# A new order for the list of steps of a banded-attention and mixture-of-experts kernel

## The chip, the cores and the metric

The kernel runs on one core of a Trainium2 chip. A core has five engines that work side by side, each through its own instructions in order: TensorE (PE in the profile, PEld for its weight loads), VectorE (DVE), ScalarE (ACT), GpSimd (POOL) and SyncE (SP). Loads and stores are issued by a queue of POOL, SP or ACT and are carried by 16 DMA engines. The metric is device time in microseconds (us), the median of several executions.

## The reference

Eight batches, eight heads, 576 positions, head size 64. Attention looks back at most 63 positions; its output, heads side by side, is the input of a layer of experts that is chosen once per batch by a gate on the mean over the positions.

```python
scores = scale * np.matmul(q, k.transpose(0, 1, 3, 2))     # (8, 8, 576, 576)
mask = (rel >= 0) & (rel < 64)                             # rel = row - column
attn = softmax(np.where(mask, scores, -1e9))
x = np.matmul(attn, v)                                     # heads side by side: (8, 576, 512)
...
pooled = x.mean(axis=1)
logits = pooled @ w_gate                                   # 8 experts
e_idx = np.argmax(logits, axis=1)                          # one expert for a batch
h = np.maximum(x[mask] @ w1[e], 0.0)                       # w1: 512 x 1024
out[mask] = gate_w[mask, None, None] * (h @ w2[e])         # w2: 1024 x 512
```

## The kernel before

Everything is issued from one list of short names, `OPS`. The loop at the end of the kernel walks through it and calls one function for each name, and no other scheduling takes place. The list therefore sets the order of instructions on every engine and in every queue: an engine works through its own steps in the order in which they stand in the list, and where a step has to wait, all that stands behind it on the same engine waits too.

The attention of a batch is cut into five units: four pairs of heads over the first 512 positions ("main" units, numbers 5b to 5b+3 for batch b) and one unit for the last 64 positions of all heads (the "tail", number 5b+4). The names, with unit or batch number behind the letter:

- `Q` loads q (even number 2b) or k (odd, 2b+1) of batch b on POOL's queue, cast to bf16 on the way, 512 KB as stored. For batch 0 a suffix names a range of heads (`Q0.48` is q, heads 4 to 7). `Y` loads two heads in fp32 on SP and `C` casts them. `t` loads both tails (two DMAs on POOL). `L` loads a fifth of a batch's v on POOL, `L5b` to `L5b+3` 128 KB each and `L5b+4` the tail, and `V` makes the copy of v that is shifted by 64 positions (two VectorE copies, lines 150 and 151).
- `T` transposes q and k of a unit on TensorE, `U` and `k` copy the transposed q and k out of PSUM, `S` makes the scores, `E` the exponential on ScalarE. The band mask is either a factor, `K` (VectorE, line 297), or, where the name of S has a `b` (`Sb`, `Smb`), two products on TensorE that add a large negative number first (line 269).
- `l` makes the row sums on TensorE, `n` and `R` their logarithm and reciprocal on ScalarE, `A` the product with v, `X` its scaling on VectorE with the sum for the mean.
- `g` and `j` are the gate's product, `G` its maximum and index on VectorE (line 404), `H` and `I` the gate's weight. `P` reads the index into a register of POOL; only then can `W4b` and `W4b+1` (the halves of w1, columns 0 to 511 and 512 to 1023) and `W4b+2` and `W4b+3` (the halves of w2) be loaded, 512 KB each as stored.
- `c` is the next piece of the expert layer on TensorE. They come in a fixed order, 18 for a batch, and this text counts them from c0: c(18b) to c(18b+7) are the eight column blocks of w1 (line 461; the first four need `W4b`, the others `W4b+1`), c(18b+8) is its tail (line 470), then two halves for each of four row blocks of w2 (line 503; the first half needs `W4b+2`, the second `W4b+3`), and the tail (line 512). `ra` or `rd` evacuates the oldest piece that is done, on ScalarE or on VectorE; `O` stores the oldest finished output on POOL's queue, `o` on SP's (the tail's second half then on ACT's).

A letter `a` or `d` inside a name picks ScalarE or VectorE for a copy; an `m` lets T, S or A use one of the three PSUM buffers of the expert layer in place of its own one. The row sums of all units and the gate share one PSUM buffer (`lb`), so an `l` waits until `n` has read the one before. q and k have buffers for three batches, the weights for three, v for three.

POOL's queue carries all loads of q, k, v and the weights and nearly all stores. Its order before, up to the weights of batch 0, is: Q0.48 Q1.48 Q0.2 Q1.2 Q3 t0 Q2 L0 L3 L1 L2 L4 t1 Q4 L9 Q5 L5 L7 L8 L6 t2 Q6 Q7 P0 W0 L12 W1 W2 L13 W3 L11 L14 L10.

## Time and profile before

| | us |
|---|---|
| median of 3 executions (203.06 to 203.96) | 203.13 |
| profiled execution, first to last instruction (span) | 201.9 |
| TensorE busy | 183.5 |
| ScalarE busy | 131.8 |
| VectorE busy | 119.9 |
| POOL busy | 111.0 |
| first expert product (c0) starts | 40.84 |
| last expert product ends | 197.6 |

The profile gives the span of the execution that it was taken from, and not its device time; the median of the executions stands 1.2 us above that span. In its rows the first number is the start or the busy time in us, then come engine, source line, operation, and the tiles written and read; "x40" counts instructions, and brackets tell how long the engine sat idle and what ended that. Rows of DMA issues give size and the time from issue to landing. Busy time of TensorE includes the pipelining of its products, so it is not a measure of how well it is used; the start-to-start distance of products is.

### The profile page before, as it was taken

How to read it: one execution, taken by the hardware profiler on the slowest of the kernel's cores; microseconds unless marked ns; L12 is line 12 of the kernel's file. 1: busy time of each engine (PE TensorE's matmuls, PEld its weight loads, DVE VectorE, ACT ScalarE, POOL GpSimd, SP SyncE). 2: the span in 40 equal slices, each digit the busy share in tenths (PEclk: the TensorE clock that was granted, in tenths of full speed). 3: DMA queues.
4: the chain of work that ended last, by engine and by line, in shares of the span. 5: the costliest groups of instructions: out<-in, count | busy, mean ns of one | idle time of the engine just before them, and what ended most of it. 6: DMA issues, size and time to landing. Idle time of an engine off the chain costs nothing.

```text
span 201.9 us, 8105 instructions
## 1 busy us (share of the span) xinstructions
PE 183.5 (91%) x3518; PEld 124.2 (62%) x3522; DVE 119.9 (59%) x347; ACT 131.8 (65%) x247; POOL 111.0 (55%) x158
## 2 busy tenths in 40 slices
PE   0487886899999999999999999999999999999991
PEld 0455564656677756577667666676656666776760
DVE  3527989595477546895877457966494651216410
ACT  2179998876599578977779975757787436321121
POOL 7985939235931593478633552439452716553561
PEclk9999999999999999999999999999999999999998
DMA  6999999999999999999999999999999999999693
GB/s 135 175 188 159 194 162 198 199 198 174 196 201 197 170 198 193 174 201 167 200 206 200 169 195 223 259 208 137 183 237 243 266 254 212 274 212 301 235 325 134
DMA packets 83346, 41.16 MB, mean 204 GB/s; under 512 B 48080, under 2 KB 80976, under 8 KB 83312
## 3 DMA queue, kind: packets, MB, share of 16 engines
q0 software_dynamic: 81936, 39.72, 138.5%
q1 hardware_dynamic: 768, 0.85, 1.3%
q8 instruction: 27, 0.44, 0.8%
q10 hardware_dynamic: 608, 0.08, 0.2%
q14 instruction: 7, 0.06, 0.1%
HBM read 61.88 MB, written 9.44 MB: 353 GB/s over the span
## 4 chain that ended last, share of the span: by engine, by line
PE 77%; DMA 9%; POOL 7%; issue 3%; DVE 2%; ACT 1%; POOLq 0%; DVEq 0%; ACTq 0%
PE ph L461 28%; PE po L503 25%; DMA vw<-in_v_dram 9%; PE tp L225 5%; PE ph L470 4%; PE s L275 4%; PE av L331 3%; PE po L512 3%; PE lb L309 3%; POOL vw L141 2%; POOL km L110 2%; POOL qm L110 1%; POOL out_dram L492 1%; PE gps L392 1%; POOL qkt L133 1%
## 5 line engine op out<-in xcount | busy, mean ns | idle before, releaser
L503 PE MATMUL po<-w2b,hm 128*64 128x512 f16 x512 | 60.1, 379 | 0.0
L461 PE MATMUL ph<-xm,w1b 128*64 128x512 f16 x512 | 60.0, 379 | 0.0
L461 PEld LDWEIGHTS <-w1b 128*64 128x64 f16 x512 | 31.7, 110 | 18.7 <-issue 0.4
L503 PEld LDWEIGHTS <-hm 128*64 128x64 f16 x512 | 30.1, 110 | 19.3
L141 POOL DMA_DIRECT2D vw<-in_v_dram x32 | 28.9, 910 | 13.3 <-DMA w1b<-in_moe_w_dram 4.3
L446 ACT ACTIVATE hm<-ph,gw 128x512 f16<-128x512 f32 x39 | 26.6, 693 | 13.4 <-PE ph L461 13.3
L492 POOL DMA_DIRECT2D out_dram<-ob x31 | 17.2, 557 | 25.0 <-DMA w1b<-in_moe_w_dram 7.0
L351 ACT ACTIVATE ln<-lb 128x512 f32<-128x512 f32 (+1 forms) x40 | 22.5, 563 | 11.8 <-PE lb L309 8.6
L364 DVE CUSTOM_DVE_ANT_0 xm<-av,rl 128x512 f16<-128x512 f32 x32 | 21.6, 686 | 10.4 <-PE av L331 9.5
L482 ACT COPY ob<-po 128x512 f32<-128x512 f32 x18 | 10.6, 586 | 23.6 <-PE po L503 23.6
L448 DVE TENSOR_SCALAR hm<-ph,gw 128x512 f16<-128x512 f32 x25 | 18.7, 748 | 12.1 <-PE ph L461 11.6
L357 ACT ACTIVATE rl<-ln 128x512 f32<-128x512 f32 (+1 forms) x40 | 23.3, 594 | 1.5 <-DVE pool L364 1.3
L225 PE MATMUL tp<-ident,qm 128*64 128x128 bf16 x256 | 13.8, 232 | 7.4 <-DMA qm<-in_q_dram 6.9
L288 ACT ACTIVATE pe<-s 128x1024 f16<-128x1024 f32 x19 | 19.5, 1028 | 1.4 <-PE s L275 0.7
L297 DVE TENSOR_TENSOR pe<-pe,mask 128x1024 f16<-128x1024 f16 x24 | 16.3, 687 | 3.9 <-ACT pe L288 3.1
L252 ACT COPY kT<-tp 128x512 bf16<-128x512 bf16 x19 | 11.2, 597 | 9.0 <-PE tp L225 8.0
L225 PEld LDWEIGHTS <-qm 128*64 128x64 bf16 x256 | 10.7, 118 | 10.0 <-DMA qm<-in_q_dram 6.9
L482 DVE COPY ob<-po 128x512 f32<-128x512 f32 x14 | 9.7, 690 | 10.7 <-PE po L503 10.5
L423 POOL DMA_DIRECT2D w1b<-in_moe_w_dram x16 | 12.6, 785 | 5.9 <-DMA vw<-in_v_dram 2.9
L275 PEld LDWEIGHTS <-kT 64*128 64x128 bf16 x576 | 10.1, 95 | 8.9 <-issue 5.6
L331 PEld LDWEIGHTS <-vw 128*64 128x64 f16 x512 | 12.4, 112 | 4.7 <-issue 1.2
L225 PE MATMUL tp<-ident,km 128*64 128x128 bf16 x256 | 13.9, 231 | 1.4 <-DMA km<-in_k_dram 0.9
(80 smaller groups left out, 267.2 us busy)
## 6 DMA issues: line engine op xcount, KB each, us to landing
w1b<-in_moe_w_dram POOLq DMA_DIRECT2D x16, 512.0 KB, 9.3
w2b<-in_moe_w_dram POOLq DMA_DIRECT2D x16, 512.0 KB, 13.4
out_dram<-ob POOLq DMA_DIRECT2D x31, 256.0 KB, 8.1
vw<-in_v_dram POOLq DMA_DIRECT2D x32, 128.0 KB, 9.0
km<-in_k_dram POOLq DMA_DIRECT2D x7, 512.0 KB, 9.3
qm<-in_q_dram POOLq DMA_DIRECT2D x7, 512.0 KB, 9.0
out_dram<-obt POOLq DMA_DIRECT2D x14, 64.0 KB, 7.7
qkt<-in_q_dram POOLq DMA_DIRECT2D x8, 64.0 KB, 7.6
```

Of the source, the lines that this page charges most:

```text
L141: nc.gpsimd.dma_start(out=vt[:, 2 * J + 1], in_=v[b, :, 128 * J:128 * J + 128].rearrange("h c d -> c h d"))
L225: nc.tensor.transpose(tp[p0:p0 + 64, n, r], t[:, 2 * i + hh, ts(r, 64)], ident)
L288: nc.scalar.activation(out=po, in_=sp[0], func=AF.Exp, scale=scale)
L351: nc.scalar.activation(out=ln, in_=lb[:, 0:n], func=AF.Ln)
L357: nc.scalar.activation(out=rl, in_=lns.pop((b, i)), func=AF.Exp, scale=-1.0)
L364: nc.vector.tensor_tensor_reduce(out=xm[:, i], in0=av.rearrange("q r p -> q (r p)"), in1=rl, scale=1.0, scalar=0.0, op0=ALU.mult, op1=ALU.add,
L446: nc.scalar.activation(out=o, in_=i, func=AF.Relu, scale=g)
L448: nc.vector.tensor_scalar(out=o, in0=i, scalar1=g, scalar2=0.0, op0=ALU.mult, op1=ALU.max)
L461: nc.tensor.matmul(out=ph[64 * c:64 * c + 64], lhsT=w1t[:, kb, ts(2 * ft + c, 64)], rhs=xm[:, kb], start=(kb == 0), stop=(kb == 3), skip_g ...
L482: copy(e)(out=ob, in_=po)
L492: (nc.scalar if n and eng is nc.sync else eng).dma_start(out=dst, in_=src)
L503: nc.tensor.matmul(out=po[64 * c:64 * c + 64], lhsT=hm[:, fb, ts(2 * r + c, 64)], rhs=w2t[:, fb], start=(fb == 0), stop=(fb == 7), skip_gr ...
```

## The change

The list is replaced by another one with the same steps; nothing else in the kernel changes. Every step of before is there once, with these differences: nine S with mask products on TensorE become three (units 0, 7 and 9), and their units, with others exchanged, get a `K` (37 in place of 31); 12 evacuations go from `ra` to `rd` (ra 65 to 53, rd 47 to 59); ten `U` go from VectorE to ScalarE, two `k` the other way; one of the two casts C goes to ScalarE; nine S and two A less, and one T more, use the expert layer's PSUM; three stores go from POOL's queue to SP's (`o` 2 to 5).

The order on every engine is new. On POOL, up to the weights of batch 0 and a little beyond: Q0.48 Q1.48 (identity) t0 Q1.2 Q2 (band) Q0.2 Q3 L2 L1 L3 L0 Q5 L4 t1 Q4 L7 L5 L8 L6 Q7 t2 P0 W0 L9 W1 Q6 L13 L10 L11 L12 W2 W3. Stores begin between W9 and L22 of that queue, where before they began behind W17.

```diff
 OPS = (
-    "Y0.24 Q0.48 Q1.48 Q0.2 Cd0.24 y i Q1.2 Y1.24 Q3 Cd1.24 z Tm3 Tm2 mb T0 Tm1 ka3 ka2 ka0 "
-    "t0 Ud3 Ud2 Q2 Sb3 L0 L3 ka1 L1 L2 E3 Smb2 L4 Ud0 l3 Ud1 t1 S0 T4 E2 kd4 Ud4 n3 Smb1 E0 "
-    "Mb K0 E1 R3 Q4 L9 Tm5 Sb4 Tm7 Tm8 Ud5 Q5 ka5 kd8 E4 L5 kd7 l1 n1 T6 l4 n4 Ud7 l2 Sb5 ka6 "
-    "n2 R1 R4 l0 V0 A3 Ud6 L7 Am1 n0 E5 T9 X3 Am2 Ud9 S7 R2 L8 E7 Ud8 X1 R0 l5 X2 L6 n5 Smb6 "
-    "A0 Am4 K7 ka9 E6 t2 X4 X0 Sb8 l7 g0 n7 T12 j0 Q6 Sm9 Tm10 G0 Ud12 kd12 E8 Ud10 H0 E9 "
-    "Tm13 Tm11 R7 K9 l6 R5 ka10 Sb12 Ud11 ka13 V1 n6 Q7 l8 P0 Ud13 W0 I0 kd11 T14 Am5 A7 X7 "
-    "A6 Ud14 kd14 L12 n8 X5 E12 R6 l12 n12 Sm14 X6 S11 l9 E14 Smb10 Tm17 E11 n9 T18 W1 Ud17 "
-    "A9 W2 E10 S13 kd18 Ud18 L13 Tm15 Ud15 l10 Am8 R8 W3 kd15 ka17 T16 K14 L11 c X8 L14 n10 "
-    "E13 R9 c ra X9 c R10 c rd c g1 K11 rd S17 j1 G1 ra ra c H1 L10 c rd l14 K13 c t3 ra c P1 "
-    "n14 Q8 ra c c rd c V2 Ua16 c c ra ka16 l11 A10 X10 Am12 W4 c Q9 R12 X12 n11 ra W5 R11 "
-    "A11 rd W6 T19 E17 c l13 n13 R13 Ua19 I1 X11 c Sm18 S15 K17 L15 rd E18 W7 R14 A13 c l17 "
-    "ra X13 A14 c L16 L17 X14 g2 n17 Tm20 E15 ra kd19 c Ud20 ra L18 kd20 T22 S19 Sm16 E19 L19 "
-    "j2 G2 c P2 t4 K15 E16 Q10 K18 c ra c W8 H2 ra ka22 c ra c c S20 l18 ra rd rd K16 c n18 "
-    "Q11 K19 L21 ra Tm21 c c Ua21 Ud22 l16 W9 T23 R17 kd21 L23 V3 c c R18 c ra Am17 Ud23 n16 "
...
-    "I6 l39 W27 R38 c n39 O O A38 rd R39 c W25 W26 ra X39 X38 g7 c j7 O c G7 c ra c P7 rd ra "
-    "c c O W29 O c ra c O rd H7 O ra c O c W28 W31 ra O ra O c ra c c ra rd c c c c rd c W30 "
-    "I7 O ra O c rd c c ra rd O c O O rd c O rd O O c rd c c O ra c c rd c O rd ra rd c c O "
-    "rd O c c ra O O c c c c ra rd o O c ra O c ra o "
+    "Q0.48 Q1.48 Y1.24 i t0 Tm3 Q1.2 Ua3 Ca1.24 kd3 Tm2 Y0.24 T4 Q2 Cd0.24 Ud2 Sm3 y ka2 Tm1 "
+    "Q0.2 mb E3 Ud1 ka1 S2 Tm0 E2 K3 Q3 kd4 Ua0 kd0 Sm1 l3 z Sb0 K2 E1 n3 Ud4 L2 Tm7 L1 L3 L0 "
+    "Q5 l2 E0 T5 ka7 L4 K1 t1 Tm6 Ua7 Mb n2 l1 Q4 R3 kd6 S4 Ua5 L7 kd5 n1 V0 Smb7 E4 l0 L5 R2 "
+    "A3 Ud6 K4 L8 T8 n0 X3 L6 E7 Am2 R0 S5 l4 Q7 A1 E5 Am4 Am0 X2 X0 n4 S6 Ud8 R4 l7 kd8 T9 "
+    "Tm13 K5 R1 X4 n7 l5 Tm12 E6 X1 g0 S8 n5 ka9 R7 E8 Tm11 ka13 j0 Ud12 K6 G0 R5 H0 Ua9 l6 "
+    "Ua13 t2 kd12 V1 Ua11 A7 K8 Sm12 T10 P0 S13 n6 l8 X7 A5 E12 E13 kd11 kd10 Ud10 W0 n8 L9 "
+    "Smb9 W1 Q6 E9 R6 I0 T14 X5 S10 Am6 L13 A8 K12 X6 l12 R8 c E10 L10 c c rd ka14 n12 L11 K10 "
+    "l9 R12 rd n9 R9 c c L12 K13 l10 W2 X8 S11 ra Am9 rd W3 c ra n10 c Q8 X9 Ua14 g1 j1 rd G1 "
+    "E11 rd H1 K11 P1 c S14 ra R10 Tm17 Tm18 Ua17 l11 kd17 T15 Ua18 E14 V2 c Ud15 S17 ka18 Am10 "
+    "n11 kd15 A12 c X12 W4 ra Q9 l13 E17 T16 Am13 K14 t3 n13 S18 l14 A11 X10 c rd R13 W5 c c "
+    "n14 c L14 E18 Ud16 ra X13 c kd16 t4 c c R11 rd K18 K17 c l17 X11 rd W6 S16 n17 c E16 W7 I1 "
+    "c T19 rd c ka19 rd l18 ra R14 rd c Tm23 ra Ua19 c n18 A14 Ud23 ka23 L16 ra c X14 ra g2 L17 "
+    "c K16 j2 c Tm21 R17 G2 S15 L15 rd c ra E15 Ud21 kd21 L18 P2 c S19 c rd T24 Tm20 c K15 E19 "
+    "ka20 c L20 Q10 S21 rd H2 Q11 l16 V3 A17 c Ua20 ka24 c R18 X17 Ua24 n16 W8 T22 A18 I2 l15 "
+    "rd E21 L19 R16 K19 rd Sm20 L24 K21 L23 n15 S23 X18 c E20 A16 c X16 K20 Ua22 W9 E23 l19 O "
+    "rd ka22 c n19 Tm26 T28 Ud26 c ra kd26 l20 Ud28 kd28 n20 S26 ra Am19 R19 R15 X19 c A15 T27 "
+    "X15 l21 L22 rd E26 ka27 n21 c rd c K23 R21 L21 S24 c K26 ra E24 V4 c t5 K24 S22 l23 ra R20 "
+    "ra c c g3 ra n23 c Ud27 W10 W11 l24 n24 ra A21 ra X21 c T29 Am20 c ra kd29 j3 Q12 O G3 E22 "
+    "H3 Ua29 c R23 c I3 S28 l26 X20 Q13 E28 c c L27 R24 A24 P3 K22 X24 L28 Am23 n26 S27 l22 ra "
+    "E27 c X23 c ra A22 W12 n22 c K27 Tm25 rd ra L26 Ud25 T32 ka25 Tm30 L25 W13 W15 S29 kd30 "
+    "E29 Ud30 c c ra K28 L29 R26 R22 ra V5 W14 c X22 c rd l27 n27 g4 kd32 S25 Ua32 ra c A26 j4 "
+    "E25 c G4 T31 H4 rd S32 Ud31 X26 K29 l28 R27 c rd n28 A27 c ra R28 I4 L35 c c rd E32 kd31 c "
+    "O ra l29 L31 S30 K25 rd n29 c c t6 ra c X27 c A28 l25 P4 n25 Q14 c c ra E30 T33 c R25 ka33 "
+    "K30 ra L30 W16 rd c l30 S31 R29 Ua33 Am25 O L33 T34 K32 X28 W17 c rd Ud34 Q15 A29 ra n30 "
+    "X25 c E31 c c X29 S33 l32 n32 g5 rd rd L32 kd34 c E33 O T36 O W18 c W19 rd j5 O Ua36 c L36 "
+    "V6 O A32 rd R32 S34 kd36 t7 T35 O R30 ra L34 G5 E34 H5 rd c O P5 c K31 Tm37 K34 l34 n34 "
+    "S36 ra X32 Ud37 W20 W22 c K33 kd35 A30 I5 ra c E36 c l31 R34 X30 ka37 Ud35 n31 T38 R31 S37 "
+    "Sm35 l33 rd Ud38 c c O E35 c ka38 n33 K36 R33 K35 c l35 rd ra W21 O c A31 c n35 rd ra X31 "
+    "E37 Am33 R35 c O A34 rd c l36 X33 ra X34 L38 T39 S38 c ra g6 L37 c n36 c ra j6 rd c G6 rd "
+    "c Ua39 E38 rd c O c ka39 H6 K38 W23 c c V7 S39 K37 l37 n37 c rd E39 rd O c O rd l38 A37 O "
+    "R37 X37 c P6 Am35 I6 c X35 rd c c R36 rd rd n38 W27 K39 W24 R38 W25 c A38 c c rd O X38 "
+    "Am36 ra rd O X36 l39 L39 O O n39 O c c A39 W26 O R39 ra X39 c ra O g7 c O j7 rd G7 H7 ra c "
+    "c c ra rd P7 c I7 ra W28 c W29 c c ra O O c ra c c ra c rd O c W30 rd c O rd c ra c O rd c "
+    "W31 rd c O c c rd O O O c ra c rd c rd O ra c c c ra c c o rd c o c rd o o ra o "
 ).split()
```

## The prediction

> **What bounds the kernel now.** I read the busy line, the table by stage, the chain of waits, then the DMA issues with their time to landing, one by one.

> ```profile
> span 201.9 us, 8105 instructions
> PE 183.5 (91%) x3518; PEld 124.2 (62%) x3522; DVE 119.9 (59%) x347; ACT 131.8 (65%) x247; POOL 111.0 (55%) x158
> HBM read 61.88 MB, written 9.44 MB: 353 GB/s over the span
> ...
> 30.00:40.00 10.00, 7.38 (x223) 5.61 (x221) 7.14 (x19) 8.86 (x17) 6.46 (x8) 1.00 1.48 198
> 40.00:60.00 20.00, 20.00 (x388) 12.72 (x384) 13.67 (x40) 13.84 (x27) 10.98 (x13) 1.00 1.52 192
> 195.00:201.90 6.90, 2.61 (x33) 1.82 (x28) 0.69 (x1) 0.96 (x2) 1.08 (x2) 0.88 0.52 186
> ...
> 22.68 8.52 DMA vw<-in_v_dram
> ...
> 1.46 0.88 POOL L110 DMA_DIRECT2D qm<-in_q_dram  x1 [0.82 <-POOLq L578]
> 40.84 4.48 PE L461 MATMUL ph<-xm,w1b 128*64 128x512 f16 x40
> 196.54 1.07 PE L512 MATMUL po<-w2b,ht 128*64 128x256 f16 x16
> ```

> TensorE has gaps until the first expert product (c0) at 40.84 us; from 40 on it has none until its last product ends at 197.6, and 4.3 us of evacuation and store follow. So the span is c0's start, plus TensorE's work after it, plus any stall, plus 4.3. The executions' median, 203.13, is 1.2 us above the profiled span; I add 1.2.

> Ahead of c0 the DMA queue decides: 8.5 us of the chain are the wait for L6, the last of batch 1's V, which lands at 31.2. Three 512 KB loads, one 128 KB load, and the POOL entry eight places behind W0 (the rows with a start are issues; those without give size and time to landing, in the same order):

> ```profile
> 25.22 0.88 POOL L110 DMA_DIRECT2D qm<-in_q_dram  x1
> 27.82 0.88 POOL L110 DMA_DIRECT2D km<-in_k_dram  x1 [1.72 <-DVE grd L384]
> 30.04 0.75 POOL L423 DMA_DIRECT2D w1b<-in_moe_w_dram  x1 [1.34 <-DVE kT L252]
> 30.78 0.89 POOL L141 DMA_DIRECT2D vw<-in_v_dram  x1
> 40.09 0.88 POOL L141 DMA_DIRECT2D vw<-in_v_dram  x1 [2.27 <-DMA w1b<-in_moe_w_dram]
> ...
> qm<-in_q_dram POOLq DMA_DIRECT2D x1, 512.0 KB, 9.0
> km<-in_k_dram POOLq DMA_DIRECT2D x1, 512.0 KB, 9.0
> w1b<-in_moe_w_dram POOLq DMA_DIRECT2D x1, 512.0 KB, 9.4
> vw<-in_v_dram POOLq DMA_DIRECT2D x1, 128.0 KB, 9.5
> ```

> Q6 lands at 34.2, Q7 at 36.8, W0 at 39.4, L12 at 40.3: one behind the other, 2.6 us for 512 KB and 0.86 for 128 KB, whatever their issue times. The queue is a saturated line. Worked out from landings in the same way, a V tail costs 0.47, each of the two tail loads of a t 0.42, a stored row block 0.63, a half tail store 0.18; a weight quarter 2.55, a whole Q 2.62. And POOL keeps at most eight in flight: L10 is issued when W0, eight places before it, has landed.

> **The change part by part.** Prices on TensorE come from the chain, where it ran without a gap (eight chunks of each kind; one unit of the others), and one mask product pair from the timeline:

> ```profile
> 166.21 6.90 PE ph L461 x64
> 173.11 0.99 PE ph L470 x62
> 174.10 6.94 PE po L503 x64
> 181.04 0.87 PE po L512 x16
> 70.35 0.45 PE tp L225 x16
> 45.33 0.34 PE s L275 x16
> 72.52 0.22 PE lb L309 x2
> 75.78 0.25 PE av L331 x16
> 12.86 0.60 PE L269 MATMUL s<-maskb,ident 128*128 128x512 bf16 x2
> ```

> A W1 chunk is 0.86, its tail 1.0, a W2 half 0.87, its tail 0.87; T 0.45, S 0.34, l 0.22, A 0.25; tail units about half of that, gate products as an l.

> *Mask additions on TensorE, nine before, three after.* All of them, old and new, lie ahead of c0, where TensorE waits for loads, so the 6 x 0.6 us that go are worth nothing by themselves. Six more multiplications K land on VectorE instead.

> *Moved behind c0.* TensorE did 16 whole T, 12 S, 10 l before c0; the new order does 12, 11 and 9, and a tail less of S, l and A. That is 4 x 0.45 + 0.34 + 0.22 + 0.4 = 2.8 us more after c0. Summing every entry after c0: 155.4 us before (it took 156.8, so 1.4 of small stalls), 158.2 after. Hence c0 has to come 2.8 us sooner before anything is won.

> *The first gate.* The V shift of batch 0 begins at 20.34, when L0 to L3 have landed; ahead of them stand the same loads in both orders (Q0 to Q3, t0), so it stays. What VectorE does from there to the gate:

> ```profile
> 20.34 0.89 DVE L150 COPY vw<-vw 64x2048 f16<-64x2048 f16 x1 [0.54 <-DMA vw<-in_v_dram]
> 28.64 0.16 DVE L404 FIND_INDEX8 eidx<-gmx,gps 128x8 uint32<-128x8 f32 x1
> ...
> L297 DVE TENSOR_TENSOR pe<-pe,mask 128x1024 f16<-128x1024 f16 x24 | 16.3, 687 | 3.9 <-ACT pe L288 3.1 <-ACT pe L291 0.5
> L252 DVE COPY kT<-tp 128x512 bf16<-128x512 bf16 x13 | 8.8, 684 | 2.8 <-PE tp L225 1.9 <-ACT qt L242 0.9
> ```

> The new order adds K4 (half a K, 0.35), kd8 (0.68) and, after g0, K6 (0.69); K5 stands for K7 and Ud12 for Ud9. 1.7 us in all. The gate's index, 28.8 before (28.64 + 0.16), stays at 28.8 if waits of VectorE in this stretch take all of that up, at 30.5 if none; I take 30.0, nearer the full price, because the additions stand ahead of the last X and of the gate product. It is later, not sooner.

> *W0 and c0.* Ahead of W0 in the queue the new order has one whole Q (Q6) and one V tail (L9) less: 2.62 + 0.47, so the line would deliver it at 36.3. Its issue comes 1.2 us after the index, as before (28.80 to 30.04), at 31.2. A fresh 512 KB load has landed in as little as

> ```profile
> qm<-in_q_dram POOLq DMA_DIRECT2D x1, 512.0 KB, 6.7
> ```

> so 37.9 at most by that row, which itself still stood in line. Between 36.3 and 37.9 I take 37.0, and c0 at 37.1. TensorE can be there: V1 can shift when L6 lands (31.2 before, one V tail less ahead of it, so 30.7; the two copies take 1.8), and from its end at 32.5 TensorE has 3.6 us of work to c0. ScalarE is the doubt, in a rival below. So c0 comes 3.7 us sooner, 2.8 of it is paid back in moved work: 0.9 is left.

> *The load line after W0.* This is where I expect it to be lost. Up to W23 the new order queues 23 W, 9 Q, 24 L, 6 V tails, 10 tail loads, 12 row stores and 4 half tail stores behind W0: 58.7 + 23.6 + 20.6 + 2.8 + 4.2 + 7.6 + 0.7 = 118.2 us. The old one has 22 W, 8 Q, 24 L, 6, 10, 7 stores and 2: 109.5. What the old line really took, with W16 as a half-way mark, and the W2 pair c99, c100 of batch 5:

> ```profile
> 114.06 0.75 POOL L423 DMA_DIRECT2D w1b<-in_moe_w_dram  x1 [0.46 <-DMA vw<-in_v_dram]
> 141.71 0.79 POOL L426 DMA_DIRECT2D w2b<-in_moe_w_dram  x1
> ...
> w1b<-in_moe_w_dram POOLq DMA_DIRECT2D x1, 512.0 KB, 9.3
> w2b<-in_moe_w_dram POOLq DMA_DIRECT2D x1, 512.0 KB, 12.1
> ...
> 157.58 1.73 PE po L503 x16
> ```

> W16 landed at 123.4, 84.0 after W0, where the sum says 82.0; W23 at 153.8, 114.4 after W0 against 109.5. So the line loses 2.0 us up to W16 and 4.9 to W23 by itself. Before, that cost nothing: c100, which needs W23, started at 158.4, 4.6 us after it. In the new order c100 comes 117.8 us of work after c0: 37.1 + 117.8 + 1.2 of small stalls = 156.1. W23 lands at 37.0 + 118.2 = 155.2 with no loss at all, 157.2 with the loss to W16, 160.1 with all of it. I take the first 2.0 and half of the rest, 3.5: 158.7, and TensorE waits 2.6 us. The same sums give W8 no cover (37.0 + 43.9 + 1.0 = 81.9 against c36 at 37.1 + 43.8 + 0.3 = 81.2) nor W19, so the wait should build up in pieces from about 75 us on; it is the largest of the shortfalls, not their sum.

> *Evacuation and stores.* Twelve evacuations go from ScalarE to VectorE (0.75 against 0.69 us each), ten q copies the other way: neither engine was over 65% busy, and behind c0 their cover is TensorE's chunks. Three stores more on SP at the end are worth 0 to 0.3 us either way; the last one still waits for the last product. I put 0.

> Sum: 37.1 + 158.2 + 1.4 + 2.6 + 4.3 = 203.6 span, 204.8 us.

> [...] Single loads here read 1 MB of HBM in 2.55 us, 411 GB/s. [...]

> **The rivals.** *The line keeps up (faster).* Nothing is lost beyond what queues anyway, W0 lands at 36.3 and c0 starts at 36.4: 36.4 + 158.2 + 1.4 + 4.3 + 1.2 = 201.5. For it: up to W16 only 2.0 of 84 were lost. Against: it needs under 1 us lost to W23. It decides from W23 landing before 156.

> *It comes out even.* The line loses 2.0 in all and c0 is at 37.1: a wait of 1.1, 203.3. This is also the case in which the change gains its 3.7 us at c0 and gives them back.

> *The head comes late (slower).* ScalarE was 89% busy in 30 to 40, and the new head gives it more q copies and a cast; each l waits until it has read the l before, so a late n holds TensorE. With full durations end to end I get c0 at about 39. Then 39.0 + 158.2 + 1.4 + 1.5 + 4.3 + 1.2 = 205.6, and 207 with all of the line's loss. It decides from c0 after 38.5. The gates of batches 3 and 7 belong here: from j3 to its first product lie 9.5 us of work, before 17.5, and the product (0.2), the index (0.4), the issue (1.2), L28 (0.9) and a landing of 6.7 need 9.4.

> **How the numbers follow.** Forecast 0.4, faster rival 0.24, even 0.18, late head 0.18. 0.5% is 1.0 us, about what this kernel's measurement can tell from none. Of the forecast a sixth ends within it (little loss), of the even case all, and the faster rival lies beyond it only if c0 keeps under 36.9: 0.25 faster, 0.25 same, 0.5 slower. Range: 201.5, where the line loses nothing, to 207.0, a late head with all of the loss; the forecast's own is 203.3 (loss 2.0) to 206.3 (loss 4.9).

> **What would show it.** Right: c0 at 36.5 to 38; the first gate's index after 29; in the waits of TensorE, L461 or L503 behind w1b or w2b loads, absent before, some 2 to 3 us in all; W8 landing as c36 starts. Wrong: no such waits and no gap in the 60 to 160 stages (faster), or c0 after 38.5 behind ScalarE (late head), or a lead-out other than 4.3.

## The result, and the profile after

The new order is slower: 215.60 us median (213.77 to 218.21) against 203.55 for the order of before on the same chip, a ratio of 1.056 (95% interval 1.050 to 1.062). The ratio is taken over the executions outside a slower state that some fall into, so it is not quite that of the two medians. The prediction said 204.8, with 207.0 as its upper end. The execution with the profile below took 213.77 us, 1.6 us of it outside the span.

The head of the profile's page after the change: span, TensorE's busy time, traffic, and the chain of waits by engine and by line. The line numbers of after are one smaller than those of before, since the list is one row shorter.

```profile
span 212.2 us, 8065 instructions
PE 186.2 (88%) x3508; PEld 121.9 (57%) x3510; DVE 128.8 (61%) x356; ACT 126.6 (60%) x235; POOL 110.4 (52%) x155
HBM read 61.88 MB, written 9.44 MB: 336 GB/s over the span
...
PE 40%; DMA 35%; issue 8%; POOL 7%; DVE 4%; ACT 3%; POOLq 1%; DVEq 0%; ACTq 0%
```

The same row of the chain in the profile of before:

```profile
PE 77%; DMA 9%; POOL 7%; issue 3%; DVE 2%; ACT 1%; POOLq 0%; DVEq 0%; ACTq 0%
```

The chain that sets the end was three quarters TensorE, and is now 40% TensorE, 35% transfers, and 8% "issue", in which the profile names no cause. The table by stage (busy time of each engine, then TensorE's granted clock, DMA share and GB/s) says where:

```profile
30.00:34.00 4.00, 1.47 (x46) 1.10 (x46) 3.87 (x11) 4.00 (x11) 1.78 (x2) 1.00 0.97 95
34.00:38.00 4.00, 4.00 (x94) 2.71 (x90) 3.31 (x9) 2.94 (x7) 4.00 (x6) 0.57 1.23 150
...
40.00:60.00 20.00, 18.47 (x378) 11.85 (x374) 14.21 (x40) 14.31 (x28) 8.21 (x11) 1.00 1.52 194
80.00:100.00 20.00, 18.91 (x422) 12.81 (x420) 13.79 (x37) 15.00 (x28) 7.85 (x10) 1.00 1.52 202
...
180.00:200.00 20.00, 19.03 (x298) 13.28 (x296) 7.54 (x17) 5.23 (x10) 9.65 (x17) 1.00 1.10 223
```

Before, TensorE was busy for 20.00 of the 20 us from 40 to 60, and its granted clock was 1.00 from 12.6 to 200.3 us. Now it has gaps in that stage and in nearly every later one, and ahead of them stands a stretch, 34 to 38, in which it works at 0.57 of its clock.

The head, from the timeline (start, duration, engine, line; brackets: idle time before, and its end):

```profile
29.85 0.29 PE L391 MATMUL gps<-grd,ones 128*64 128x8 f32 x4
29.95 0.68 DVE L296 TENSOR_TENSOR pe<-pe,mask 128x1024 f16<-128x1024 f16 x1
30.83 0.16 DVE L403 FIND_INDEX8 eidx<-gmx,gps 128x8 uint32<-128x8 f32 x1
31.96 0.30 ACT L431 ACTIVATE gex<-gps,gnm 128x8 f32<-128x8 f32 x1
32.22 1.17 POOL L422 DMA_DIRECT2D w1b<-in_moe_w_dram  x1 [5.65 <-DVE kT L251]
32.40 0.41 PE L308 MATMUL lb<-pe,ones 128*64 128x512 f16 x2 [2.27 <-ACT gex L431]
38.57 2.76 PE L460 MATMUL ph<-xm,w1b 128*64 128x512 f16 x24
```

The gate's index ends at 31.0, W0 is issued at 32.2 after POOL has stood still for 5.65 us, and it lands at 38.08. TensorE stands still for 2.27 us, because the next row sums (l6) share the PSUM buffer with the gate's product and wait until ScalarE's exponential has read it; in the new list nothing for TensorE stands between the two, where before Sm9, Tm10, Tm13 and Tm11 did. Then the granted clock is 0.5 from 34.16 to 37.58 us, and c0 starts at 38.57: sooner than before by 2.3 us, which is less than the 2.8 us of work that was moved behind it.

Behind c0 TensorE needs 169.8 us, up to the end of its last product at 208.4. Its work there is 158.2 us by the prediction's prices, so it loses 11.6 us, where before it lost 1.4. TensorE's rows with a wait, from the timeline:

```profile
50.70 0.63 PE L330 MATMUL av<-pe,vw 128*64 128x64 f16 x28 [0.51 <-DVE vw L150]
53.89 0.36 PE L224 MATMUL tp<-ident,km 128*64 128x128 bf16 x6 [0.86 <-issue]
75.70 0.25 PE L224 MATMUL tp<-ident,qm 128*64 128x128 bf16 x2 [0.39 <-issue]
82.72 0.38 PE L274 MATMUL s<-qt,kT 64*128 64x64 bf16 x14 [0.88 <-issue]
88.91 0.22 PE L338 MATMUL al<-pp,vw 128*64 128x64 f16 x2 [0.21 <-issue]
118.33 0.41 PE L274 MATMUL s<-qt,kT 64*128 64x64 bf16 x16 [0.56 <-ACT pe L287]
159.31 1.92 PE L460 MATMUL ph<-xm,w1b 128*64 128x512 f16 x16 [0.70 <-DMA w1b<-in_moe_w_dram]
165.40 1.92 PE L502 MATMUL po<-w2b,hm 128*64 128x512 f16 x16 [0.47 <-DMA w2b<-in_moe_w_dram]
183.71 7.10 PE L502 MATMUL po<-w2b,hm 128*64 128x512 f16 x64 [0.97 <-DMA w2b<-in_moe_w_dram]
201.29 6.23 PE L502 MATMUL po<-w2b,hm 128*64 128x512 f16 x56 [0.82 <-DMA w2b<-in_moe_w_dram]
207.33 1.07 PE L511 MATMUL po<-w2b,ht 128*64 128x256 f16 x16
```

Laid against the summed work, unit by unit, the 11.6 us come in these steps: 1.4 at 50.7 to 51.5 (the shifted V of batch 2, then c9 whose weight W2 landed at 51.34); 3.4 at four stops inside a unit with no releaser ("issue"; 1.07, 0.62, 1.19 and 0.49 with what queues behind them); 3.6 at four weights (0.99 for W21, 0.54 for W23, 1.03 for W26, 1.01 for W31); 1.3 at two waits for a producer (110.7 and 118.3); and 1.9 in steps of under 0.4 (one of them, 0.38 at 101.95, is a stop of the same kind as the four, as the counts below show). The weights are late where POOL had been held by a gate, or waited for the landing eight places before. POOL's rows:

```profile
102.17 0.88 POOL L140 DMA_DIRECT2D vw<-in_v_dram  x1 [8.20 <-DVE gnm L406]
117.79 0.88 POOL L109 DMA_DIRECT2D qm<-in_q_dram  x1 [2.94 <-DVE gnm L406]
163.76 0.76 POOL L425 DMA_DIRECT2D w2b<-in_moe_w_dram  x1 [2.22 <-DVE hm L447]
183.22 1.55 POOL L422 DMA_DIRECT2D w1b<-in_moe_w_dram  x2 [3.10 <-PE ph L469]
193.03 0.78 POOL L425 DMA_DIRECT2D w2b<-in_moe_w_dram  x1 [3.49 <-PE ph L460]
```

The first four stand right behind a P (P3, P4, P6, P7); the releaser named is what the gate's index came with. The last is W31, issued as W29, eight places before it, landed at 192.38.

### The profile page after: what moved, and what is told of

Same layout as the page of the kernel before. It is cut to its first block, busy times and chain, and to the rows that moved or that the text cites. A ratio compares the mean times of both kernels' runs of the same rounds, so it can differ in the third digit from the quotient of the medians.

```text
span 212.2 us, 8065 instructions
## 1 busy us (share of the span) xinstructions
PE 186.2 (88%) x3508; PEld 121.9 (57%) x3510; DVE 128.8 (61%) x356; ACT 126.6 (60%) x235; POOL 110.4 (52%) x155
## 3 DMA queue, kind: packets, MB, share of 16 engines
HBM read 61.88 MB, written 9.44 MB: 336 GB/s over the span
## 4 chain that ended last, share of the span: by engine, by line
PE 40%; DMA 35%; issue 8%; POOL 7%; DVE 4%; ACT 3%; POOLq 1%; DVEq 0%; ACTq 0%
PE po L502 16%; DMA w2b<-in_moe_w_dram 12%; DMA w1b<-in_moe_w_dram 11%; PE ph L460 10%; DMA vw<-in_v_dram 9%; DMA qm<-in_q_dram 3%; PE tp L224 3%; PE s L274 3%; PE av L330 2%; PE po L511 2%; PE lb L308 1%; POOL vw L140 1%; POOL qm L109 1%; POOL w1b L422 1%; PE ph L469 1%
## 5 line engine op out<-in xcount | busy, mean ns | idle before, releaser
L460 PEld LDWEIGHTS <-w1b 128*64 128x64 f16 x512 | 28.1, 110 | 19.8 <-DMA w1b<-in_moe_w_dram 1.7
L447 DVE TENSOR_SCALAR hm<-ph,gw 128x512 f16<-128x512 f32 x33 | 24.6, 747 | 11.1 <-PE ph L460 10.7
L445 ACT ACTIVATE hm<-ph,gw 128x512 f16<-128x512 f32 x31 | 21.1, 687 | 16.3 <-PE ph L460 16.3
L287 ACT ACTIVATE pe<-s 128x1024 f16<-128x1024 f32 x26 | 26.7, 1025 | 2.9 <-PE av L330 1.9
L296 DVE TENSOR_TENSOR pe<-pe,mask 128x1024 f16<-128x1024 f16 x30 | 20.3, 682 | 6.3 <-ACT pe L287 5.5
L425 POOL DMA_DIRECT2D w2b<-in_moe_w_dram x16 | 12.4, 774 | 16.5 <-DMA w1b<-in_moe_w_dram 4.0
L481 DVE COPY ob<-po 128x512 f32<-128x512 f32 x17 | 11.7, 688 | 14.7 <-PE po L502 14.5
L251 DVE COPY kT<-tp 128x512 bf16<-128x512 bf16 x19 | 12.9, 683 | 11.9 <-ACT qt L241 11.5
L481 ACT COPY ob<-po 128x512 f32<-128x512 f32 x15 | 8.8, 587 | 16.6 <-PE po L502 16.6
L274 PEld LDWEIGHTS <-kT 64*128 64x128 bf16 x576 | 11.6, 98 | 12.3 <-issue 9.4
L274 PE MATMUL s<-qt,kT 64*128 64x64 bf16 x512 | 13.7, 197 | 2.7 <-ACT pe L287 1.3
## 6 DMA issues: line engine op xcount, KB each, us to landing
w1b<-in_moe_w_dram POOLq DMA_DIRECT2D x16, 512.0 KB, 9.4
w2b<-in_moe_w_dram POOLq DMA_DIRECT2D x16, 512.0 KB, 9.6
vw<-in_v_dram POOLq DMA_DIRECT2D x32, 128.0 KB, 8.9
qm<-in_q_dram POOLq DMA_DIRECT2D x7, 512.0 KB, 8.5
km<-in_k_dram POOLq DMA_DIRECT2D x7, 512.0 KB, 10.4
```

The costliest lines, as they stand in the source:

```text
L274: nc.tensor.matmul(out=sp[hh][:, ts(m, 64)], lhsT=kq, rhs=qt[p0:p0 + 64, m], start=not pm, stop=True, skip_group_check=True)
L287: nc.scalar.activation(out=po, in_=sp[0], func=AF.Exp, scale=scale)
L445: nc.scalar.activation(out=o, in_=i, func=AF.Relu, scale=g)
L447: nc.vector.tensor_scalar(out=o, in0=i, scalar1=g, scalar2=0.0, op0=ALU.mult, op1=ALU.max)
L460: nc.tensor.matmul(out=ph[64 * c:64 * c + 64], lhsT=w1t[:, kb, ts(2 * ft + c, 64)], rhs=xm[:, kb], start=(kb == 0), stop=(kb == 3), skip_g ...
L481: copy(e)(out=ob, in_=po)
```

## The experiments

**Half an order at a time.** Is the loss in POOL's queue (theory L) or in the order on the engines (theory T)? Two lists each combine POOL's queue of one order with all other engines' order of the other. Their first difference is this:

```diff
 h_newc_oldp, POOL's queue
-... Q7 t2 P0 W0 L9 W1 Q6 L13 L10 L11 L12 W2 W3 Q8 P1 W4 ...
+... t2 Q6 Q7 P0 W0 L12 W1 W2 L13 W3 L11 L14 L10 t3 P1 Q8 W4 ...
 h_oldc_newp, POOL's queue: the reverse
```

> The changed order of every other engine, with POOL's queue (loads, register reads, stores) in the order of before. Theory L (the loss of 10 us lies in POOL's queue: weights and V arrive late because stores and other loads stand ahead of them): c0 near the landing of W0 as before, 40 us, no waits of TensorE for weights, 204 to 207 us. Theory T (it lies in the order of TensorE and the engines that feed it: waits inside units that no load ends): 211 us or more, and TensorE lags behind its own work by 5 us or more after c0 without any wait for a weight load.

> The order of before on every engine, with the changed order of POOL's queue alone. Theory L: the weights of batches 5 to 7 land late again, 208 to 213 us. Theory T: the gates come at their old places ahead of the weights, TensorE waits 1 to 3 us for weights at most, 203 to 206 us.

Measured: 239.77 us (235.49 to 242.38) for the first; 231.97, ratio 1.138 (1.133 to 1.143), for the second. Both theories fail: the second's time is far over both ranges, and the first's is far over theory L's, while its TensorE waits for weights, which theory T excluded. TensorE's waits in the first:

```profile
PE tp L226 <- DMA qm<-in_q_dram: 13.8, 2, 7.3
PE ph L462 <- DMA w1b<-in_moe_w_dram: 10.9, 3, 5.4
```

After c0 the first needs 191.1 us, and the second 176.3, each in its profiled execution (238.35 and 234.63). What follows: an order of POOL's queue belongs to one order of compute. A queue that reaches P before its gate is done stands still (8.20 us behind P3 in POOL's rows of the new order), and what stands behind P then comes late for another engine. The two lists can't be judged apart, so I looked for single causes inside the new one.

**Stores ahead of the weights.** The new order begins its stores sooner. Here each store on POOL goes back to its old place relative to the weight loads:

```diff
-... P5 W20 W22 O W21 O O L38 L37 O W23 O O O P6 W27 W24 W25 O O L39 O O O W26 O O O P7 W28 ...
+... P5 O O O W20 O W22 O W21 L38 L37 W23 P6 O O W27 O O W24 O O W25 L39 W26 P7 O O W28 ...
```

> The changed kernel with the output stores moved back in POOL's queue, so that as many stand ahead of each weight load as before (none ahead of W18; the five SP stores at the end unchanged). Theory L: the 7 to 12 stores that no longer stand ahead of W20 to W23, 0.63 us each, bring these 4 to 7 us sooner, TensorE's waits at c94, c100 and c117 (2.5 us) go, 210 to 212. If the late weights come from late gates and not from the stores ahead of them: same as the changed kernel within 1 us.

Measured: 223.47 us, ratio 1.099 (1.092 to 1.106), 8 us worse than the new order. TensorE's longest wait, and POOL's:

```profile
PE ph L461 <- DMA w1b<-in_moe_w_dram: 7.1, 4, 3.9
```

```profile
POOL out_dram L492 <- DVE hm L448: 21.0, 4, 12.8
POOL out_dram L492 <- ACT gex L432: 14.2, 1, 14.2
```

With fewer stores ahead of it POOL reaches P6 and P7 earlier and stands there longer; the stores that were taken away then stand between the gate and its weights. In the new order the stores filled time in which POOL would have waited anyway. So taking stores from ahead of a P does not bring its weights sooner here. The edit also puts stores between a P and its W; that this is the place that counts is my reading of the two long waits, and no run changes it alone.

**The later gates taken away.** From the second batch on, the register load reads a constant zero (so these batches take the weights of expert 0, and the gate's choice is left out); in the second kernel the order of before gets the same edit.

```diff
+    zidx = gpool.tile([128, 8], U32, tag="zidx", name="zidx", bufs=1)
+    nc.gpsimd.memset(zidx, 0)
...
-        nc.gpsimd.load(ereg, eidxs[b][0:1, 0:1])
+        nc.gpsimd.load(ereg, (eidxs[b] if b == 0 else zidx)[0:1, 0:1])
```

> The new order, but from the second batch on the register load takes a constant zero in place of the gate's index (so batches 1 to 7 load the weights of expert 0: that part of the computation is changed), so GpSimd's queue never stands still for a later gate. Theory feedback (late gates hold GpSimd, that makes weights late, that holds TensorE, that makes the next gate late): the waits of the expert products for weights (about 3.6 us) and for V and W2 (1.4 us) go, and with them what follows; of the 11.5 us that TensorE falls behind its work after the first expert product 4 to 6 are left (instruction fetch 2.5 to 2.9, producers); time 206 to 209.5. Theory line (the DMA line moves 300-odd GB/s and is simply full, whenever the gates come): the same waits return at the same products, time 213 to 216.

> The same edit on the order of before (batches 1 to 7 load the weights of expert 0), as the control. Both theories: its TensorE loses only 1.3 us after the first expert product and waits for no weights to speak of, so 202.3 to 204.5; if it gains over 1 us, late gates cost the order of before too, unseen in its waits.

Measured: 210.24 us, ratio 1.032 (1.027 to 1.037), for the new order, and 203.99, ratio 1.002 (0.999 to 1.004), for the old one. The end of x_nogate (first and last expert product, and a stage):

```profile
38.49 2.76 PE L462 MATMUL ph<-xm,w1b 128*64 128x512 f16 x24
203.95 1.07 PE L513 MATMUL po<-w2b,ht 128*64 128x256 f16 x16
...
160.00:180.00 20.00, 20.00 (x332) 12.09 (x330) 15.59 (x44) 8.50 (x18) 11.25 (x18) 1.00 1.12 233
```

From c0 to the end of the last product it takes 166.5 us, 3.3 less than the new order, and all of that is gained after 150 us: at 143 to 145 us it is as far behind its work as the new order (7.5 us). One wait for a weight of 0.3 us is left. So it is shown that the later gates hold POOL and make the weights late, which is worth 3.3 us in the profiled executions and 5.4 between the medians; a full load line is not the cause. That a late weight makes the next gate late in turn follows from the order of the steps and was not tested by itself. But 8.3 us of loss remain, theory feedback had left 4 to 6, and its 206 to 209.5 us were missed. The control loses nothing: the old order's gates are early enough.

**The first gate taken away as well.**

```diff
-        nc.gpsimd.load(ereg, (eidxs[b] if b == 0 else zidx)[0:1, 0:1])
+        nc.gpsimd.load(ereg, zidx[0:1, 0:1])
```

> As x_nogate (210.2 us), but the register load of the first batch takes the constant zero too (all batches load the weights of expert 0), so GpSimd never stands still for a gate, the first one included, and the load line doesn't run dry at 31 to 34 us. Theory head (the dry stretch of the first gate is what makes V of the third batch and the second weight late, and the 1.4 us lost at 50.7 to 51.5 us are its price): the first expert product starts when TensorE gets to it, at 37.0 to 37.8 (38.5 now), the 1.4 us go, the instruction stops stay; time 207 to 208.8. Theory order (what TensorE loses before 150 us is in the order itself: short waits for producers and instruction stops, whatever the loads do): 209.4 to 210.6.

Measured: 210.72 us, ratio 1.032 (1.026 to 1.038). Theory order all but holds (its range ended at 210.6), theory head falls.

```profile
32.88 0.41 PE L308 MATMUL lb<-pe,ones 128*64 128x512 f16 x2 [2.26 <-ACT gex L433]
39.33 2.76 PE L462 MATMUL ph<-xm,w1b 128*64 128x512 f16 x24
203.86 1.07 PE L513 MATMUL po<-w2b,ht 128*64 128x256 f16 x16
```

W0 is now issued at 28.0 and lands at 37.2, 0.9 us sooner, and c0 still starts at 39.33. Here W0 did not hold c0: TensorE got there no sooner, after the same stop of 2.26 us and the same 3.4 us at half clock. The V shift at 50 us costs the same again (0.8), and behind c0 7.4 us are still lost.

**The head's stop.** Three tries to shorten it. x_gate0 moves the first gate's steps up; x_gate0w also puts eight products of zeros into the stop; x_gcopy copies every gate's product to SBUF first, so that `lb` is free at once.

```diff
 x_gate0
-j0 Ud12 K6 G0 R5 H0
+j0 G0 H0 Ud12 K6 R5
 x_gate0w, beside that
-l6
+F8 l6
 x_gcopy
-j0 Ud12 K6 G0 R5 H0
+j0 G0 Ud12 K6 R5 H0
...
-        glog = gpss.pop(b)
+        glog = gpool.tile([128, E], FP32, tag="glog", name="glog")
+        nc.vector.tensor_copy(out=glog, in_=gpss.pop(b))
```

> The new order with the first gate's index and its exponential moved ahead of the copy of Q for unit 12, the mask of unit 6 and the reciprocals of unit 5. The index comes 0.4 to 0.7 us sooner (30.9 now), the first weight's load at 31.6 to 31.8 (32.2 now), TensorE's stop before the sums of unit 6 shrinks from 2.3 us to 1.0 to 1.5. Theory feedback: what is gained in the head is gained at every later gate, time 1 to 2.5 us under the new order's, 211.5 to 214.5. Theory line: the load line starts its weights sooner but is as full, under 0.7 us.

> x_gate0 and eight products of constant zeros (1.7 us) on TensorE just ahead of the sums of unit 6, in the stop. If it is the stop that brings the granted clock down to 0.5 from 34 to 37.7 us, the clock stays near 1.0 there, and the products up to the first expert product take 1.5 to 2 us less; the first expert product then waits for its weight alone (37.3 to 38.1). Time as x_gate0 or up to 1 us under it. If the clock falls all the same, the stop isn't its cause, and the time is 0 to 1.5 us over x_gate0.

> The new order with two edits that keep the result: every gate's product is copied from the accumulator to SBUF by VectorE as its first step (8 numbers per row, an estimate of 0.1 to 0.2 us from the 0.16 us maximum), so that the buffer that the row sums share is free at once; and the first gate's steps on VectorE stand ahead of the copy of Q for unit 12 and the mask of unit 6. TensorE's stop between the first gate's product and the sums of unit 6 (2.27 us in the new order) shrinks to 0.7 to 1.3 us, bounded by the mask of unit 6. Theory clock (a stop of about 2 us halves the granted clock for some 3 us, and that, not the weight, holds the first expert product): no drop of the granted clock at 32 to 38 us, the first expert product 7.5 to 8.0 us after the start of the first gate's product (8.7 in the new order), then bound by its weight; time 0.5 to 1.5 us under the new order's, 212.5 to 215. Theory weight: the first product still comes 8.5 us or more behind the gate's product, whatever the clock; time as the new order's.

Measured: 216.82 (213.68 to 217.22), 217.05 (213.62 to 219.08) and 216.75 us (214.72 to 218.19): none is better than the new order, and x_gate0w is inconclusive, since its eight products themselves waited 2.13 us, for a copy by VectorE, and so did not fill the stop. In x_gate0 the index ended 0.77 us after the start of the gate's product in place of 1.14, but TensorE's stop only shrank to 1.75 (1.0 to 1.5 expected), and the copies of V, now later, stopped it for another 0.64 and 0.45. One stage of x_gcopy, and TensorE's waits:

```profile
34.00:38.00 4.00, 3.49 (x82) 2.79 (x78) 3.49 (x8) 1.64 (x4) 4.00 (x6) 0.52 1.25 150
...
32.28 0.41 PE L309 MATMUL lb<-pe,ones 128*64 128x512 f16 x2 [1.71 <-DVE pe L297]
33.79 0.25 PE L331 MATMUL av<-pe,vw 128*64 128x64 f16 x4 [1.10 <-DVE vw L150]
34.55 0.53 PE L331 MATMUL av<-pe,vw 128*64 128x64 f16 x12 [0.51 <-DVE vw L151]
41.16 2.76 PE L462 MATMUL ph<-xm,w1b 128*64 128x512 f16 x24
```

The wait for ScalarE is gone, and VectorE holds TensorE instead: first the mask of unit 6, then the two copies of V, one behind the other in a queue that is busy for 3.87 of the 4 us from 30 to 34 in the new order. The clock now stays halved for 6.8 us in place of 3.4, and c0 comes 10.9 us behind the gate's product, 2.2 us later than in the new order (8.7). The stop did not shrink as the clock theory said, and the copies of V add 1.6 us of stops, so this run does not part the two theories.

Three kernels do, because their order up to c0 is the same on every engine and the clock differs: x_stores, the new order and x_fill (below). The stop is 2.26 or 2.27 us in each. The first three rows are of x_stores, the last two of x_fill:

```profile
33.08 0.41 PE L309 MATMUL lb<-pe,ones 128*64 128x512 f16 x2 [2.26 <-ACT gex L432]
34.00:38.00 4.00, 3.80 (x144) 2.98 (x140) 3.90 (x10) 3.66 (x9) 4.00 (x6) 1.00 0.87 121
38.86 1.49 PE L461 MATMUL ph<-xm,w1b 128*64 128x512 f16 x12 [0.45 <-DMA w1b<-in_moe_w_dram]
...
34.00:38.00 4.00, 4.00 (x78) 2.79 (x72) 3.32 (x9) 2.40 (x5) 4.00 (x6) 0.50 1.23 148
39.41 2.76 PE L462 MATMUL ph<-xm,w1b 128*64 128x512 f16 x24
```

From the start of l6 TensorE needs 5.3 us until it is ready for c0 in x_stores, where the clock never fell in the head; 6.2 in the new order, with 3.4 us of half clock (6.2 to 6.5 in x_nogate, x_nogateall and x_fetch64, with as much); and 7.0 in x_fill, with 6.8. So each 3.4 us of half clock costs some 0.8 us. At full clock it is the weight that holds c0, by 0.45 us in x_stores. In the new order TensorE would have been ready at 37.7 (an estimate: 32.40 and the 5.3 of x_stores), and W0 landed at 38.08: the half clock put c0 off by 0.5 us beyond its weight.

**The stops without a releaser.** Count what TensorE was given ahead of each of them: weight loads, products, and the semaphore and drain steps of its queue. The counts are 1729, 2498, 2754 and 3010, each 193 or 194 more than a multiple of 256 (the 202 in an expectation below comes of counting the semaphore and drain steps twice). The trace has 27 DMA packets of 16 KB on a queue named "instruction", and TensorE goes on 1.4 to 1.6 us after the end of one. Theory: the instructions arrive in blocks of 256, and a stretch of short instructions (T, S and A take 32 in 0.45, 0.34 and 0.25 us, a chunk of an expert product 16 in 0.86) uses a block up before the next is there. x_fetch64 and b_fetch64 put 64 small products ahead of everything, so that the ends of the blocks fall 128 instructions earlier in the code; x_fill lengthens the stretch ahead of two stops.

```diff
 x_fetch64, b_fetch64
+    "F64 ...
-                    nc.tensor.matmul(out=wps, lhsT=warm[:, 0:128], rhs=warm, start=True, stop=True)
+                    nc.tensor.matmul(out=wps[0:64, 0:64], lhsT=warm[:, 0:64], rhs=warm[:, 0:64],
+                                     start=True, stop=True)
 x_fill
+REPEAT = {13: 3, 15: 3}
-        for hh in range(2):
+        for hh in [0, 1] * REPEAT.get(5 * b + i, 1):
```

> The changed kernel with 64 small products (128x64, output unused) ahead of everything on TensorE, in the time in which it waits for the first load: 128 more instructions. In the changed kernel TensorE stands still inside a unit, waiting for nothing that the profile names, at 53.9, 75.7, 82.7 and 88.9 us, always at the same place modulo 256 of its instructions. If that is the fetching of its instructions in blocks of 256, these four stops (2.3 us) vanish from T16, T20, S23 and A19 and stops appear half a block away or not at all; if they belong to the units (a buffer, a producer that the profile does not name), they stay where they are, at the same units. Time 212 to 217 either way.

> The order of before with 64 small products of constant zeros ahead of all (128 TensorE instructions, so the ends of the instruction blocks fall 128 instructions earlier in the code). Theory instruction fetch: the one stop it has (0.50 us at 38.7) goes or moves, and others may appear wherever a block now holds a dense stretch; the order of before has few of them, so 0 to 2 us in all, 203.3 to 205.5; each stop at a count of 202 more than a multiple of 256. If no stop moves, the theory falls.

> The new order with the row sums of units 13 and 15 each written three times instead of once (the same numbers into the same place), so TensorE gets 2 x 0.82 us of extra work just ahead of its stops at 53.0 us (0.86) and 81.8 us (0.88). Theory instruction fetch (a block of 256 TensorE instructions arrives at its own time, and a dense stretch runs out before it comes): the stops shrink to 0.0 to 0.3 us each and the extra work is free: TensorE is as far behind at the expert products after them as in the new order, within 0.4 us, and the time is the new order's (213.5 to 216). Theory producers (the stops are a late operand that the trace doesn't name): an operand's time doesn't depend on it either, so the stops shrink as well, but it then must be the operand of just those instructions; the block's end is told by the place: the stop sits at the same count of instructions, so 8 and 16 instructions earlier in the code. If neither holds, each stop stays and the time rises by 1.6 us.

Measured: x_fetch64 217.69 us, ratio 1.069 (1.065 to 1.072); b_fetch64 206.33, ratio 1.011 (1.005 to 1.016); x_fill 215.97, ratio 1.055 (1.048 to 1.062). One row of x_fetch64, one of b_fetch64, two of x_fill:

```profile
51.71 0.35 PE L276 MATMUL s<-qt,kT 64*128 64x64 bf16 x12 [1.83 <-issue]
```

```profile
40.90 0.19 PE L331 MATMUL av<-pe,vw 128*64 128x64 f16 x1 [1.46 <-issue]
```

```profile
54.84 0.25 PE L226 MATMUL tp<-ident,qm 128*64 128x128 bf16 x2 [0.99 <-issue]
83.24 0.50 PE L276 MATMUL s<-qt,kT 64*128 64x64 bf16 x22 [0.62 <-issue]
```

In x_fetch64 the four stops are gone from their units, and new ones of 1.83, 1.66 and 1.63 us stand in other units (51.7, 57.8 and 146.8 us) at counts 1730, 1985 and 5313. (The profile puts the second down to a copy on VectorE; the count, and a packet's end 1.4 us before it, put it at a block's end.) In b_fetch64 the old order's one stop (0.50 us at count 1218) is gone, one of 1.46 us stands at 1474, and smaller ones at 3010, 3522 and 3777 (the last, 0.53 us, put down to ScalarE): 2.35 us slower between the medians, a little past the range expected, for 64 products that lie in TensorE's idle start (the first gate's product starts at 27.6, before at 28.0). In x_fill the two stops again stand at 1729 and 2754, so 8 and 16 instructions earlier in the code. They did not shrink to 0.0 to 0.3 us, as was expected: they last 0.99 and 0.62 (0.86 and 0.88 in the new order). The extra work was mis-sized in the expectation: four more products of 512 columns take 0.40 us, not 0.82. Counted from c0, TensorE passes the first stop 0.11 us later than in the new order (15.43 against 15.32) and the second 0.32 sooner, since the stop at 75.7 went too; so 0.8 us of extra work was free. The place of the stop follows the count, and its end follows a packet (1.3 to 1.6 us after the packet's end for each stop named here): instruction fetch is shown. What decides when a block's packet starts stays open: ahead of the new order's stops and the old order's one it started 2.4 to 4.6 us after the end of the block before, over all blocks of these two traces 0.2 to 4.7.

## Why the prediction was wrong

**The first gate.** "I take 30.0" for the index: 31.0, past the full price of 30.5. The gate's product came 1.8 us later than before, where the additions ahead of it had been priced at 1.0; the rest was not taken apart. Behind it K6, the third addition, stands in VectorE's queue between the product and the maximum and costs 0.4 more.

**W0 and c0.** W0 was issued at 32.2 (31.2 predicted), 1.2 us after the index as said, and landed at 38.08 (37.0). c0 started at 38.57 (37.1). Two steps failed here. One is the index, taken 1.0 us too early, which puts W0 off by 1.1. The other is "TensorE can be there ... it has 3.6 us of work to c0": V1's copies ended at 33.08, not 32.5, and from there it took 5.5 us. x_stores took 4.6 for the same at full clock, so of the 1.9 too much some 0.9 is the half clock, and 1.0 was not taken apart. Either step alone would have made c0 late: x_nogateall, with W0 0.9 us sooner, gains nothing, and x_stores, with TensorE 0.8 us quicker, waits for W0. The rival of the late head named ScalarE and the shared `lb`, and its bound, c0 after 38.5; that part came true, with the gate's exponential as the reader. It knew nothing of the clock, though, and its 205.6 to 207 missed the rest.

**Moved work.** 158.2 us behind c0 was not the failure: between the losses TensorE keeps to the summed work. Even with c0 as measured and no loss at all the end would have been 38.57 + 158.2 = 196.8, later than 40.84 + 155.4 = 196.2 of before: the sooner first product was paid back in moved work, as predicted, and 0.5 us more, where 0.9 had been predicted to be left.

**"1.4 of small stalls".** This is the largest failure. It was carried over from before, and 7.4 to 8.3 us are lost with no gate and almost no weight in the way: in the new order's steps 3.4 at block ends of the instruction fetch (3.8 with the one at 101.95), 0.8 to 1.4 at the V shift, and some 3 at short waits for producers, of which two of 0.5 to 0.8 us are named by the profile and the rest lies in steps of under 0.4 whose causes I did not separate. The trace of before had shown the first kind once, 0.5 us at 38.7, put down to "issue". I had summed it up among the stalls and not asked what it was.

**The load line, "the largest of the shortfalls, not their sum".** 2.6 us were predicted, and 3.6 are lost at weights: the size was nearly right, and place and mechanism were not. The waits stand at 159, 165, 184 and 201 us, not from 75 on (W8 landed at 85.94, 4.0 us later than predicted, and c36 started at 86.9, 5.7 later, without a wait). The line was taken as a saturated one that starts at W0 and runs by itself. It stands still whenever POOL waits at a P, and the gate waits for TensorE; TensorE's own losses therefore come back as late weights, and each wait adds to the one before. x_nogate takes the gates away and the waits go with them.

**Small terms.** Evacuation, stores and masks at 0: no run took the masks apart, and in x_stores other places of the stores cost 8 us, so they are not worth 0, but that run moves them on both sides of the gates. Lead-out 3.8 (4.3 predicted), outside the span 1.6 (1.2). The sum as measured: 38.57 + 158.2 + 11.6 + 3.8 + 1.6 = 213.8. The low end of the range, 201.5, was not put to the test: no run of the new list came near it, and its span moved 336 GB/s.

## What to carry to other kernels

A sooner first product is worth nothing until the work that was moved behind it is subtracted (here 2.3 us sooner, 2.8 us moved); then ask of each queue that waits for a result, what its lateness will make late next, and whether that comes back to it: with the later gates away x_nogate took 3.3 us less behind c0. Between a product whose PSUM buffer is read slowly and the next that needs the buffer, leave TensorE other work: here the stop was paid twice, with 2.27 us of idle time and with 3.4 us of half clock, some 0.8 us more. A stop of TensorE inside a unit with no releaser is to be looked up by its count of instructions: in this kernel stretches of transposes and small products used a block up fastest (32 instructions in 0.25 to 0.45 us, against 16 in 0.86 for a chunk), and 0.8 us of longer products set into two of them cost x_fill nothing. An order that looks good by its summed work can still lose time there; this one lost 3.4 us.

## What the runs showed of the hardware that I had not expected

**Instruction blocks.** TensorE's instructions came in 16 KB packets, 27 of them for 7043 instructions in the new order's trace, 261 each, and at the end of a block of 256, by the counts of the stops, it stopped for 0.2 to 1.8 us where it stopped. The four blocks of the new order that ended so had been used up in 4.4 to 6.1 us; three blocks of the old order passed in 4.7 to 4.8 us without a stop (one from 79.03 to 83.68), so no single time tells. The stops cost 3.4 us of 213.8 here, and b_fetch64, in which they moved and grew, is 2.35 us slower between the medians.

**A spread of its own.** The new order's executions lie between 213.77 and 218.21, over 2% apart. In two kernels a wait of over 2 us for a weight was followed by slower products too: in x_gate0 TensorE waits 2.27 us ahead of c136, and each of the next two chunks takes 0.8 us longer than its 0.87; in h_newc_oldp it waits 3.05 us up to 194.81, and the next chunk takes 1.71 us, at a granted clock of 0.91 over the stage 180 to 200. There a late weight cost more than its wait.
